# A fused attention, Fourier and feed-forward kernel: 13 plain attention tiles for 18, masking and weight conversion on VectorE, first Fourier rows placed by matrix products

## The chip, the cores and the metric

The kernel runs on one core of one Trainium2 chip. The metric is the device time of one execution in microseconds. The program has five engines that run beside one another, each with its own queue worked off in order: TensorE (PE; PEld is its weight load), VectorE (DVE), ScalarE (ACT), GpSimd (POOL) and the sync engine (SP), which here issues nearly all DMA transfers.

## The reference, cut to what matters

```python
# attention: 8 batches, 8 heads, 576 positions, head size 64, window of 64
scores = q @ k^T / 8, masked to 0 <= row - column < 64, else -1e9
attn = exp(scores - max) / (sum + 1e-9)
x = (attn @ v), heads put side by side          # (8, 576, 512)
# Fourier mixing and feed-forward
mixed = real(fft(fft(x, axis=1), axis=2))
u = x + mixed
un = (u - mean(u)) / sqrt(var(u) + 1e-6)
out = u + relu(un @ w_ch1) @ w_ch2              # w_ch1 512 x 2048, w_ch2 2048 x 512, float64
```

## The kernel before, in words

The 8 x 576 positions are 36 tiles of 128 rows (`NTT`); two batches make a pair of 9 tiles (`NT`). Each tile goes through `attn_tile`; when a batch is complete, `fft` transforms it, and `norm_tile` adds the Fourier rows to the attention rows and normalises them. Two tiles make a chunk, and `ffn` runs over 18 chunks.

**Plain and split tiles.** Tiles below `PRO` are plain (`whole`): scores and the product with v are float32 products, and k, q and the probabilities are transposed on PE against an identity (`flip`, L462; `flip_p`, L595). From `PRO` on, a tile is split into float16 high and low parts, multiplied in three passes or four partial products, and transposed by DMA (`k_turn`, `q_turn`, `p_turn`), with the splitting done on ACT, POOL or DVE. For a plain tile a product of an identity with the mask first puts the mask into the score bank (L542), four products add the scores (L545), DVE takes the row maximum (`top`, L573 and L574) and ACT the exponential from PSUM (L580). For a split tile DVE adds the mask and takes the minimum in one custom instruction a head pair (`masked`, L564).

**Order.** Every step is an `op` with an engine, a guessed duration and a priority. `Plan.order` simulates the engines with those guesses and writes out a fixed order for each queue: whatever can start first goes first, and priority settles ties. An attention tile has a base of 8.5 T plus an offset (`EARLY` for the first five); feed-forward products have 1e6 and more, so they fill PE where nothing else is ready. `slack` pretends that inputs of PE come later than planned. Where the plan sees PE idle before the first feed-forward product, `warm` products (L1265) fill the gap. A ring of ten `xu` tiles (`XR`) holds attention rows until their chunk is done, so tile T waits for chunk (T - 10) / 2.

**Weights.** The weights arrive as float64 words in 32 pieces of 512 KB (`weight_piece`, load L1069). A piece becomes float32 by integer steps: two on DVE (L1078, L1083), one on ACT (L1088), an addition on POOL (L1091); ACT then squares it for a scale (L1095). Chunk 0 is plain: it uses the float32 weights (`PLAIN = 1`). Later chunks use float16 high and low parts that `weight_split` makes once all pieces have been seen.

**Placing the first Fourier rows.** `fft` leaves its rows in three tiles `mp` by their index modulo 3, sends them to DRAM (`send`, L927), and later norm tiles gather them from there. For the first batch, tiles 0 and 1 don't go by way of DRAM:

```python
for T in range(2):
    ...
    for a0, a1 in ((j0, j0 + 32), (j0 + 32, j1)):
        r0 = cl + 3 * a0 - P * T
        nc.sync.dma_start(mts[T][r0 : r0 + 3 * (a1 - a0) - 2 : 3], t["mp", cl][a0:a1])
    op("DMA", 1.5, base + 5.25 + 0.01 * T, direct, [bmp], [Bmt[T]], lat=3.5)
```

Those are 12 transfers on SP (L944). `stats` of `norm_tile` (L992, L994) waits for them, then come `rstd`, `scale` (L1005), `flip` (L1017), and the first feed-forward products (L1186).

**Transposed Fourier input.** `radix4` (L680) folds a tile; for plain tiles and those with n in `Y_SOON` PE transposes it (`flip_y`, L739), for the others a DMA does (`y_turn`, L754).

Of the kernel before, what the change touches and what calls it, by code (L numbers as in the profile page):

```python
# [16 lines left out]
U32 = mybir.dt.uint32  # L17
AF = mybir.ActivationFunctionType
# [6 lines left out]
DM = H * D  # L25
# [270 lines left out]
def attn_fft_ffn_kernel(ctx: ExitStack, tc: tile.TileContext, q, k, v, w1, w2, gidx, dft_d, dft_s, mask, out):  # L296
# [27 lines left out]
    idb = cp.tile([P, P], BF16, name="idb")  # L324
# [30 lines left out]
    Bid, Bmh, Bmskb, Bgix, Bdd, Bds, Bones, Bidb = (Buf() for _ in range(8))  # L355
# [6 lines left out]
    op("POOL", 0.3, -499.5, lambda: nc.gpsimd.tensor_copy(idb, ident), [Bid], [Bidb])  # L362
# [15 lines left out]
    def to_parts():  # L378

        for i in range(2):  # L380
            fresh = i == PRO % 2
# [7 lines left out]
            op("POOL", 0.7, 100, ones, writes=[Bva[i], Bve[i]] if fresh else [Bva[i]])  # L389
# [21 lines left out]
    def attn_tile(T, base):  # L411
# [29 lines left out]
        kw = 512 if whole else 1024  # L441
        kst_ = (kst32 if whole else kst16)[:, T % 3 * kw : (T % 3 + 1) * kw].rearrange("p (h s) -> p h s", s=P)

        def keys(h, jj):
# [6 lines left out]
            own, old = T % 3 * w + 2 * h, (T - 1) % 3 * w + 2 * h + 1  # L451
# [21 lines left out]
        else:  # L473
# [57 lines left out]
        for jj in range(2):  # L531
# [5 lines left out]
            def score(jj=jj, m=m):  # L537
# [19 lines left out]
            rd = [Bq[i], bkT, *([] if jj or n == 0 else [BkT[(T - 1) % 3]])]  # L557
            op("PE", 1.15 if whole else 0.6, base + 2 + jj, score, [*rd, Bidb, Bmskb] if whole else rd, [bs, bp])
# [10 lines left out]
            def top(jj=jj):  # L569

                mx, nm = (sm.tile([P, 4], F32, tag=tag, name=f"{tag}{T}_{jj}") for tag in ("mx", "nm"))
                t["nm", jj] = nm
                nc.vector.tensor_reduce(out=mx, in_=t["ps", jj], axis=AX.X, op=ALU.max)  # L573
                nc.vector.tensor_scalar(out=nm, in0=mx, scalar1=-0.125, scalar2=None, op0=ALU.mult)  # L574
# [190 lines left out]

    def fft(b, base):
# [530 lines left out]
```

## Time and profile before

| what | value |
|---|---|
| device time, median of 3 runs | 1029.38 us (1027.97 to 1029.58) |
| the profiled execution's own time | 1027.26 us |
| its span, first to last instruction | 1025.4 us |
| mean granted TensorE clock | 0.994 |
| busy: PE, PEld | 989.6 us, 709.4 us |
| busy: DVE, ACT, POOL | 676.6, 416.9, 188.5 us |
| DMA moved | 115.83 MB, mean 113 GB/s |

The execution takes 1.86 us more than its span. A PE instruction's duration contains the way through the array, and neighbours overlap; what an operation costs a full PE is the time from its start to the start of what follows. Busy times of stretches count overlaps once; sums over groups of instructions count them twice. A float32 product has two records.

### The profile page before, as it was taken

The numbers are of one execution on the slowest core, as the hardware profiler recorded it, in microseconds if no ns is written. First come the engines' busy times: TensorE is split into PE (matmuls) and PEld (weight loads), VectorE is DVE, ScalarE is ACT, GpSimd is POOL, SyncE is SP. The second block draws the span as 40 slices with busy tenths as digits, with TensorE's granted clock in tenths as the row PEclk, the third lists the DMA queues.
The fourth block names the chain that finished last, engine by engine and source line by source line (L and its number), as shares of the span: only waits on it lengthen the run. The fifth ranks groups of instructions, "written<-read, shape, count | busy, mean of one in ns | idle before, by whom it ended". The sixth has DMA issues, their size and how long they took to land.

```text
span 1025.4 us, 22178 instructions
## 1 busy us (share of the span) xinstructions
PE 989.6 (97%) x8743; PEld 709.4 (69%) x8743; DVE 676.6 (66%) x1743; ACT 416.9 (41%) x1060; POOL 188.5 (18%) x200
## 2 busy tenths in 40 slices
PE   8788999999999999989999999999999999999998
PEld 7677767677776767666676676666676667666664
DVE  5799898798756495765775757778686754532121
ACT  5777766545424263233453225343453222211111
POOL 2124432121023020311123203032112100210000
PEclk9999999999999999999999999999999999999999
DMA  8979953337238156486798456686763511220000
GB/s 196 227 187 246 228 164 108 81 74 144 58 96 159 43 100 146 90 166 106 141 134 169 108 104 114 118 174 136 127 114 88 117 20 55 62 53 21 1 22 21
DMA packets 279032, 115.83 MB, mean 113 GB/s; under 512 B 260744, under 2 KB 260872, under 8 KB 278928
## 3 DMA queue, kind: packets, MB, share of 16 engines
q1 hardware_dynamic: 276208, 105.50, 49.9%
q0 software_dynamic: 2720, 8.92, 3.2%
q8 instruction: 69, 1.13, 0.5%
q14 instruction: 35, 0.29, 0.1%
HBM read 54.97 MB, written 14.17 MB: 67 GB/s over the span
## 4 chain that ended last, share of the span: by engine, by line
PE 71%; DVE 12%; DMA 10%; ACT 2%; SPq 2%; issue 2%; POOL 1%; DVEq 0%; ACTq 0%; POOLq 0%
PE ph L1186 31%; PE po L1167 28%; PE pa L646 2%; PE pz L899 2%; PE pg L867 2%; DMA uhl<-up 2%; DMA flex<-in_moe_w_ch 2%; DMA wd<-in_moe_w_ch 2%; PE psc L552 1%; DMA pt<-flex 1%; DVE y L680 1%; DMA va<-in_v 1%; DVE hh L1204 1%; DMA mt<-md,gix 1%; PE psc L545 1%
## 5 line engine op out<-in xcount | busy, mean ns | idle before, releaser
L1186 PE MATMUL ph<-uhl,w0s 128*128 128x256 f16 (+1 forms) x3384 | 426.6, 277 | 9.4 <-DVE hh L1204 9.2
L1167 PE MATMUL po<-w1s,hh 128*128 128x512 f16 (+1 forms) x1696 | 426.8, 389 | 0.0
L1186 PEld LDWEIGHTS <-w0s 128*128 128x128 f16 x3264 | 318.1, 98 | 94.9 <-issue 13.1
L1204 DVE SCALAR_TENSOR_TENSOR hh<-ph,hh 128x256 f16<-128x256 f32 x272 | 114.8, 423 | 235.3 <-ACT hh L1201 223.0
L1201 ACT ACTIVATE hh<-ph 128x256 f16<-128x256 f32 x272 | 104.0, 382 | 401.4 <-PE ph L1186 290.1
L1167 PEld LDWEIGHTS <-hh 128*128 128x128 f16 x1632 | 157.0, 98 | 138.3 <-issue 1.1
L977 POOL DMA_INDIRECT mt<-md,gix x34 | 34.3, 1008 | 111.3 <-DMA md<-mp 90.4
L1001 POOL TENSOR_TENSOR rs<-mv,mhalf 128x1 f32<-128x1 f32 x36 | 21.8, 606 | 178.2 <-DVE mv L997 161.5
L580 ACT ACTIVATE pr<-pr,nm 128x128 f32<-128x128 f32 x144 | 45.6, 390 | 5.7 <-DVE nm L564 5.7
L580 ACT ACTIVATE pr<-psc,nm 128x128 f32<-128x128 f32 x144 | 40.4, 380 | 16.6 <-DVE nm L574 12.5
L545 PEld LDWEIGHTS psc<-kst,qbd 128*128 128x128 f32 x288 | 37.5, 192 | 5.6 <-issue 1.7
L646 PE MATMUL pa<-ve,pt 128*64 128x65 f16 (+1 forms) x720 | 40.9, 209 | 0.1
L646 PE MATMUL pa<-va,pt 128*64 128x65 f16 (+1 forms) x720 | 40.5, 209 | 0.3 <-ACT pt L403 0.2
L545 PE MATMUL psc<-kst,qbd 128*128 128x128 f32 x288 | 38.4, 277 | 1.7 <-ACT qbd L403 1.2
L609 POOL TENSOR_TENSOR flex<-pr,flex 128x512 f16<-128x512 f32 x19 | 23.0, 1215 | 91.5 <-DVE flex L407 54.2
L482 POOL TENSOR_TENSOR flex<-kn,flex 128x512 f16<-128x512 f32 x15 | 17.6, 1176 | 117.8 <-ACT flex L403 92.3
L564 DVE CUSTOM_DVE_ANT_0 pr<-psc,mskb 128x128 f32<-128x128 f32 x144 | 32.8, 285 | 1.4 <-PE psc L552 1.4
L658 DVE TENSOR_TENSOR xu<-pa,rc 128x256 f32<-128x256 f32 x72 | 30.6, 425 | 2.5
L899 PE MATMUL pz<-g,ds__76 97*96 97x257 f16 (+3 forms) x240 | 29.1, 273 | 1.6 <-ACT pr L580 1.1
L680 DVE TENSOR_TENSOR y<-xu 128x256 f32<-128x256 f32 x66 | 29.7, 491 | 1.4 <-PE py L739 0.9
L899 PEld LDWEIGHTS <-ds__76 97*96 97x96 f16 (+1 forms) x240 | 26.8, 124 | 4.2 <-issue 2.6
L403 ACT CAST up<-un 128x512 f16<-128x512 f32 x28 | 17.2, 616 | 28.2 <-DMA uhl<-up 14.3
(155 smaller groups left out, 1214.9 us busy)
## 6 DMA issues: line engine op xcount, KB each, us to landing
wd<-in_moe_w_ch SPq DMA_DIRECT2D x20, 512.0 KB, 4.1
out<-xu SPq DMA_DIRECT2D x36, 256.0 KB, 2.4
ve<-va SPq DMA_DIRECT2D x68, 130.0 KB, 3.8
kn<-in_k SPq DMA_DIRECT2D x32, 256.0 KB, 4.1
qn<-in_q SPq DMA_DIRECT2D x32, 256.0 KB
flex<-in_moe_w_ch SPq DMA_DIRECT2D x12, 512.0 KB, 4.8
md<-mp SPq DMA_DIRECT2D x24, 192.0 KB, 2.7
va<-in_v SPq DMA_DIRECT2D x16, 256.0 KB, 5.4
```

The costliest lines, as they stand in the source:

```text
L545: nc.tensor.matmul(p_[:, hp], qw, keys(hp, jj), start=False, stop=(hp == 3))
L564: nc.vector.tensor_tensor_reduce(out=t["pr", jj][:, hp], in0=t["ps", jj][:, hp], in1=mskb[:, m : m + P], scale=-0.125, scalar=3.0e38, op0= ...
L580: nc.scalar.activation(pr, src, AF.Exp, bias=t["nm", jj][:, hp : hp + 1], scale=sc_)
L646: nc.tensor.matmul(pa[64 * jj : 64 * jj + 64, hh], pt[:, sl], v_, start=(x == 0), stop=(x == len(mm) - 1))
L658: nc.vector.tensor_tensor(out=xv[:, 4 * hf : 4 * hf + 4], in0=pa[:, :, 0:64], in1=rc.to_broadcast([P, 4, 64]), op=ALU.mult)
L680: eng.tensor_tensor(out=o, in0=p0, in1=p1, op=al)
L899: nc.tensor.matmul(pz[:M, c0:c1], ds_[:NJ, a, c[0] : c[0] + c[1]], t["g", gi][:, b_, c0:c1], start=(x == 0), stop=(x == len(mm) - 1),)
L977: nc.gpsimd.indirect_dma_start(out=mts[T], out_offset=None, in_=mds[pb][0 : HR if n < 4 else 2 * HR], in_offset=bass.IndirectOffsetOnAxis( ...
L1167: nc.tensor.matmul(t["po"][i], l_, r_, start=(f == 0 and x == 0), stop=(f == NKF - 1 and x == len(mm) - 1))
L1186: nc.tensor.matmul(ph, l_, r_, start=(x == 0), stop=(x == len(mm) - 1))
L1201: nc.scalar.activation(t["hh", f][:, 0], ph, AF.Relu)
L1204: nc.vector.scalar_tensor_tensor(out=hh[:, 1], in0=ph, scalar=0.0, in1=hh[:, 0], op0=ALU.max, op1=ALU.subtract)
```

## The change

- `PRO` 18 to 13: tiles 13 to 17 become split tiles. As 13 isn't the start of a pair, keys and values of tile 12 are converted once for tile 13 (`k_tail`, `v_next`, on DVE).
- Plain tiles lose the mask product; they use `masked` on DVE like the split ones, and ACT reads the probabilities from SBUF.
- The weights' ACT and POOL steps become one DVE instruction that adds into the low 16-bit half of each word.
- The 12 transfers become six float32 products with a matrix of ones and zeros (`place3`, made once on POOL), into two PSUM banks of the ring `f2`.
- `Y_SOON` loses n = 3; `LAZY` margins, priorities, pitch (8.5 to 10), `SLACK` (1.0 from tile 18 on, now 0.5 from tile 9 on) and the weights' priorities are other numbers.

```diff
-Y_SOON = (3,4,8,)
-LAZY, LAZY_FFT, LAZY_U = 0.2, 0.8, 0.2
-LAZY_E, LAZY_Y = 0.3, 0.4
+Y_SOON = (4, 8)
+LAZY, LAZY_FFT, LAZY_U = 0.2, 0.8, 0.5
+LAZY_E, LAZY_Y = 0.3, 0.8
-EARLY, LATER = 80, 0
-PRO = 18
-SLACK = 1.0
+EARLY, LATER = 60, -20
+PRO = 13
+PITCH, FFT_AT, NORM_AT, FFT1 = 10, 10, 9, 0
+SLACK = 0.5
-W_DMA, W_DMA_STEP, W_CONV, W_SQ, W_SPLIT, W_STEP = -40, 1.25, 40, 80, 60, 0.5
+W_DMA, W_DMA_STEP, W_CONV, W_SQ, W_SPLIT, W_STEP = -20, 1.6, 40, 60, 60, 0.5
...
+        if T == PRO and n > 0:
+            def k_tail():
+                ...
+            op("DVE", 1.6, base + 0.3, k_tail, [BkT[(T - 1) % 3]], [BkT[before], Buf("tail")])
...
-                if whole:
-                    nc.tensor.matmul(p_, idb, mskb[:, None, m : m + P].to_broadcast([P, 4, P]), start=True, stop=False)
-                    nc.tensor.matmul(p_[:, hp], qw, keys(hp, jj), start=False, stop=(hp == 3))
+                    nc.tensor.matmul(p_[:, hp], qw, keys(hp, jj), start=True, stop=True)
...
-            if whole:
-                op("DVE", 0.85, base + 2.1 + jj, top, [bs], [bnm], port=False)
-                op("ACT", 1.07, base + 2.5 + jj, expo, [bs, bnm], [bp])
-            else:
-                op("DVE", 0.86, base + 2.1 + jj, masked, [bs, Bmskb], [bp, bnm], port=False)
-                op("ACT", 1.2, base + 2.5 + jj, expo, [bnm], [bp])
+            op("DVE", 0.84, base + 2.1 + jj, masked, [bs, Bmskb], [bp, bnm], port=False)
+            op("ACT", 1.18, base + 2.5 + jj, expo, [bnm], [bp])
...
-                    op("DMA", 1.5, base + 5.25 + 0.01 * T, direct, [bmp], [Bmt[T]], lat=3.5)
+        for T in range(2 if b == 0 else 0):
+            def place(T=T):
+                mts[T] = bank("f2", f"mt{T}", (P, DM))
+                for cl, M in ((1, 96), (2, 96), (0, 97)):
+                    f0 = P * T + 2 - cl
+                    nc.tensor.matmul(mts[T], place3[0][:M, f0 : f0 + P], t["mp", cl][:M], start=(cl == 1), stop=(cl == 0))
+            op("PE", 2.6, base + 5.4 + 0.1 * T, place, [*bmps, Bplace], [Bmt[T]])
...
-                nc.scalar.mul(lo, lo.bitcast(U32), 2.0**-29)
-                nc.gpsimd.tensor_tensor(out=dst, in0=dst, in1=lo, op=ALU.add)
+                half_ = wf[x][g].bitcast(U16)[:, 0::2]
+                nc.vector.scalar_tensor_tensor(
+                    out=half_, in0=lo.bitcast(U32), scalar=2.0**-29, in1=half_, op0=ALU.mult, op1=ALU.add
+                )
...
-        base = 8.5 * T + (LATER if T > 4 else -EARLY)
-        plan.slack = SLACK if T >= PRO else 0.0
+        base = PITCH * T + (LATER if T > 4 else -EARLY)
+        plan.slack = SLACK if T >= NT else 0.0
```

## Rows read from the trace of the kernel before

**Rows 1.** The page: busy time and share of the span by engine
```profile
PE 989.6 (97%) x8743; PEld 709.4 (69%) x8743; DVE 676.6 (66%) x1743; ACT 416.9 (41%) x1060; POOL 188.5 (18%) x200
```
**Rows 2.** Stages: length, busy PE, PEld, DVE, ACT, POOL, clock, DMA share, GB/s
```profile
0.00:46.00 46.00, 37.62 (x350) 31.11 (x350) 30.70 (x77) 28.09 (x74) 8.74 (x18) 0.98 0.94 211
46.00:76.00 30.00, 24.90 (x287) 21.59 (x285) 26.95 (x63) 22.68 (x61) 7.37 (x7) 0.97 0.75 194
76.00:95.40 19.40, 15.75 (x160) 13.71 (x160) 18.14 (x44) 15.44 (x43) 8.21 (x7) 0.91 0.93 237
95.40:185.00 89.60, 86.33 (x560) 64.34 (x557) 77.47 (x154) 59.51 (x149) 32.07 (x25) 1.00 0.66 166
185.00:407.00 222.00, 219.02 (x1922) 159.80 (x1923) 157.45 (x398) 97.25 (x243) 35.90 (x41) 1.00 0.48 100
407.00:853.00 446.00, 437.64 (x4295) 304.48 (x4294) 313.79 (x892) 165.95 (x418) 87.27 (x91) 1.00 0.63 118
```
**Rows 3.** Groups of PE instructions, whole span: busy, mean ns, idle before
```profile
L1265 PE MATMUL warm<-ident 128*128 128x256 f16 x103 | 17.2, 314 | 1.3 <-POOL ident masks.py:199 1.3
```
**Rows 4.** The same, 76 to 95.4 us
```profile
L1265 PE MATMUL warm<-ident 128*128 128x256 f16 x24 | 4.3, 321 | 0.0
```
**Rows 5.** The same, 0 to 95.4 us
```profile
L542 PE MATMUL psc<-mskb,idb 128*128 128x512 bf16 x18 | 6.9, 381 | 0.1
```
**Rows 6.** PE in order of time, a plain tile: start, duration, what
```profile
259.86 0.39 PE L542 MATMUL psc<-mskb,idb 128*128 128x512 bf16 x1
260.09 1.05 PE L545 MATMUL psc<-kst,qbd 128*128 128x128 f32 x8
260.98 0.60 PE L462 MATMUL pk<-ident,kn 128*128 128x128 f32 x4
261.42 0.82 PE L1186 MATMUL ph<-uhl,w0s 128*128 128x256 f16 x6
```
**Rows 7.** Chain of waits, 0 to 110 us: start, duration, what
```profile
95.52 1.92 PE ph L1186 x8
...
100.48 1.08 PE pa L646 x32
```
**Rows 8.** PE in order of time, a split tile
```profile
502.19 0.22 PE L646 MATMUL pa<-ve,pt 128*64 128x65 f16 x1
...
502.60 0.62 PE L552 MATMUL psc<-kst,qbd 128*64 128x128 f16 x16
503.14 1.48 PE L1186 MATMUL ph<-uhl,w0s 128*128 128x256 f16 x12
```
**Rows 9.** PE in order of time, two float32 products of 512 columns
```profile
168.79 1.88 PE L1167 MATMUL po<-w1s,hh 128*128 128x512 f32 x4
170.51 0.70 PE L867 MATMUL pg<-dd,fs 128*128 128x65 f16 x12
```
**Rows 10.** Line 944, the placing transfers: ns min/median/max, first and last start
```profile
L944 SPq DMA_DIRECT2D mt<-mp x12: 530/678/922, 70.9 to 81.7; - x12
```
**Rows 11.** DVE in order of time: last mixing, first addition of Fourier rows
```profile
75.81 0.16 DVE L921 TENSOR_TENSOR mp<-pz,mp 97x3 f32<-97x3 f32 x1
...
86.92 0.69 DVE L992 TENSOR_TENSOR xu<-xu,mt 128x512 f32<-128x512 f32 x1
```
**Rows 12.** Groups of DVE instructions, 0 to 95.4 us: the plain tiles' maximum
```profile
L573 DVE TENSOR_REDUCE mx<-psc 128x4 f32<-128x512 f32 x18 | 12.3, 685 | 1.6 <-PE psc L545 1.6
L574 DVE TENSOR_SCALAR nm<-mx 128x4 f32<-128x4 f32 x18 | 6.6, 367 | 0.9
```
**Rows 13.** DVE in order of time: masking of a split tile, what follows
```profile
502.07 0.28 DVE L564 CUSTOM_DVE_ANT_0 pr<-psc,mskb 128x128 f32<-128x128 f32 x1
...
502.91 1.41 DVE L1224 SCALAR_TENSOR_TENSOR xu<-po,osc,xu 128x512 f32<-128x512 f32 x2
```
**Rows 14.** Line 1083, second DVE step of a weight piece
```profile
L1083 DVE SCALAR_TENSOR_TENSOR w1s<-wd,w1s x10: 682/693/1666, 68.6 to 178.5; 128x512 int32<-128x512 int32 x10
```
**Rows 15.** Line 1091, the addition on POOL
```profile
L1091 POOL TENSOR_TENSOR w1s<-w1s,wd x10: 1288/1356/1677, 69.5 to 179.3; 128x512 int32<-128x512 int32 x10
```

More of the change, by code (lines that the diff above doesn't have):

```diff
@@ L353, in attn_fft_ffn_kernel @@
     wp = [w_[:, 0:16].bitcast(F16).rearrange("p g (z c) -> p g z c", z=2) for w_ in ws]
-    Bid, Bmh, Bmskb, Bgix, Bdd, Bds, Bones, Bidb = (Buf() for _ in range(8))
+    Bid, Bmh, Bmskb, Bgix, Bdd, Bds, Bones = (Buf() for _ in range(7))
     Bq, Bva, Bve = ([Buf() for _ in range(2)] for _ in range(3))
@@ L380, in to_parts @@
         for i in range(2):
-            fresh = i == PRO % 2
+            fresh = PRO % NT == 0 and i == PRO % 2
             def ones(i=i, fresh=fresh):
@@ L387, in ones @@
                     nc.gpsimd.memset(ve[i][64:128], 0.0)
-            op("POOL", 0.7, 100, ones, writes=[Bva[i], Bve[i]] if fresh else [Bva[i]])
+            op("POOL", 0.7, PITCH * PRO - 25, ones, writes=[Bva[i], Bve[i]] if fresh else [Bva[i]])
     def pieces(src, b0, g0, n):
@@ L441, in attn_tile @@
         kw = 512 if whole else 1024
+        before = (T + 1 if T == PRO else T - 1) % 3
         kst_ = (kst32 if whole else kst16)[:, T % 3 * kw : (T % 3 + 1) * kw].rearrange("p (h s) -> p h s", s=P)
@@ L450, in keys @@
             w = kw // 64
-            own, old = T % 3 * w + 2 * h, (T - 1) % 3 * w + 2 * h + 1
+            own, old = T % 3 * w + 2 * h, before * w + 2 * h + 1
             step = old - own
@@ L505, in attn_tile @@
                 op("DMA", TURN, base + 0.7, lambda j=j: q_turn(j), Bfl[4:6], [Bq[i]], lat=2.8)
+        if T == PRO and n > 0:
+            def k_tail():
+                src = kst32[:, (T - 1) % 3 * 512 : (T - 1) % 3 * 512 + 512].rearrange("p (a s) -> p a s", a=4)
+                dst = kst16[:, before * 1024 : before * 1024 + 1024].rearrange("p (h s) -> p h s", h=H)
+                for h in range(2):
+                    old = src[64 * h : 64 * h + 64, :, 64:128]
+                    hi, lo = (dst[64 * z : 64 * z + 64, h::2, 64:128] for z in range(2))
+                    if h:
+                        odd = sb([P, 4, 64], F32, "tail", f"odd{T}")[0:64]
+                        nc.vector.tensor_copy(odd, old)
+                        old = odd
+                    nc.vector.tensor_copy(hi, old)
+                    nc.vector.tensor_tensor(out=lo, in0=old, in1=hi, op=ALU.subtract)
+            op("DVE", 1.6, base + 0.3, k_tail, [BkT[(T - 1) % 3]], [BkT[before], Buf("tail")])
         def v_part(z):
@@ L523, in v_next @@
         def v_next():
-            nc.sync.dma_start(vbuf[3 - i][64:128], vbuf[i][64:128])
+            if T + 1 == PRO:
+                (hi, lo), v_ = (ve[1 - i][64:128, z] for z in range(2)), va32[i][64:128]
+                nc.vector.tensor_scalar(out=hi, in0=v_, scalar1=VS, scalar2=None, op0=ALU.mult)
+                nc.vector.scalar_tensor_tensor(out=lo, in0=v_, scalar=VS, in1=hi, op0=ALU.mult, op1=ALU.subtract)
+            else:
+                nc.sync.dma_start(vbuf[3 - i][64:128], vbuf[i][64:128])
         op("DMA", 0.55, base - 4 if whole else base + 3.2, v_own, [Bva[i]], [Bve[i]], lat=2.8)
-        if n + 1 < NT:
+        if n + 1 < NT and T + 1 == PRO:
+            op("DVE", 1.1, base + 6, v_next, [Bva[i]], [Bve[1 - i]])
+        elif n + 1 < NT:
             op("DMA", 0.55, base - 3.9 if whole else base + 6, v_next, [Bva[i]], [Bve[1 - i]], lat=2.8)
@@ L555, in score @@
                             )
-            rd = [Bq[i], bkT, *([] if jj or n == 0 else [BkT[(T - 1) % 3]])]
-            op("PE", 1.15 if whole else 0.6, base + 2 + jj, score, [*rd, Bidb, Bmskb] if whole else rd, [bs, bp])
+            rd = [Bq[i], bkT, *([] if jj or n == 0 else [BkT[before]])]
+            op("PE", 0.95 if whole else 0.52, base + 2 + jj, score, rd, [bs, bp])
             def masked(jj=jj, m=m):
@@ L567, in masked @@
                     )
[L569 to L574, printed above, removed]
             def expo(jj=jj):
@@ L764, in attn_tile, with make_places @@
             op(*a, port=not soon)
+    Bplace, place3 = Buf("mt"), []
+    def make_places():
+        place3.append(sb([P, 258], F32, "mt", "place3"))
+        nc.gpsimd.memset(place3[0], 0.0)
+        nc.gpsimd.affine_select(
+            out=place3[0], in_=place3[0], compare_op=ALU.not_equal, fill=1.0, base=2, pattern=[[-1, 258]], channel_multiplier=3
+        )
+    op("POOL", 0.8, -60, make_places, writes=[Bplace])
     def fft(b, base):
@@ L1033, in norm_tile @@
             op("POOL", 1.0, base, gather, [*mdr, Bgix], [bmt], lat=2.6)
-        op("DVE", 1.13 + sum(0.75 if r else 0.6 for _, _, r in RANGES[n]), base + 0.5, stats, [bmt], [bx, bst])
+        op("DVE", 1.13 + sum(0.75 if r else 0.6 for _, _, r in RANGES[n]), base + 0.5, stats, [bmt], [bx, bst], port=T > 1)
         op("POOL", 0.54, base + 0.6, rstd, [bst, Bmh], [brs])
@@ L1102, in weight_piece @@
         op("DVE", 0.6, pr - 0.1, lambda: conv(1), bw, [bf])
-        op("ACT", 0.58, pr, lambda: conv(2), bw, [br])
-        op("POOL", 1.3, pr - 0.2, lambda: conv(3), [*bw, br], [bf])
+        op("DVE", 0.6, pr - 0.2, lambda: conv(2), bw, [bf])
         op("ACT", 0.72, W_SQ + W_STEP * order, square, [bf], [bj, Bssq[x]])
```

31 lines of the change are left out of this document (11 added, 20 removed).

## The prediction

> **What bounds the kernel now.** I read the page first: PE is busy 97% of the span, DVE 66% [rows 1]. A mean over stages hides limits, so the second view is the busy time by stage [rows 2]. The reader is to see two regimes. From 95.4 to 853 us PE is busy 742.99 of 757.6 us, 98%, at a granted clock of 1.00, and no other engine comes near: there a microsecond of PE work is a microsecond of time. Before 95.4 us PE is busy 78.27 us, but 17.2 us of that (an upper value, since neighbours overlap) are warm products that compute nothing [rows 3]. So up to 17.1 + 17.2 = 34.3 of 95.4 us are no work. DVE is the full engine there: 45.1 of 49.4 us from 46 to 95.4 [rows 2]. The third view, the chain of waits, gives the point where the regimes meet: the first feed-forward products start at 95.52 [rows 7]. PE's order in time then gives what each product costs a full PE, from its start to the start of the next.
>
> **The change part by part, against the profiled execution of 1027.26 us.**
>
> *Mask products.* One costs 260.09 - 259.86 = 0.23 us [rows 6]. Two for each of 18 plain tiles make 36; 18 of them run before 95.4 us [rows 5], where PE has spare time, and I count them as nothing (at best 4.1 us). The other 18 give -4.1 us. For them DVE masks: four instructions in 502.91 - 502.07 = 0.84 us [rows 13] where the maximum took 0.69 + 0.37 = 1.05 us [rows 12]. That is 0.21 us less a group, not more.
>
> *Tiles 13 to 17.* A plain tile without its masks costs PE two score steps of 260.98 - 260.09 = 0.89 us, four groups of transposes of 261.42 - 260.98 = 0.44 us [rows 6], and 1.08 us for the product with v [rows 7]: 1.78 + 1.76 + 1.08 = 4.62 us. A split tile costs two score steps of 503.14 - 502.60 = 0.54 us and two halves of 502.60 - 502.19 = 0.41 us [rows 8]: 1.90 us. Five tiles give 5 x 2.72 = -13.6 us. What it adds is for other engines: seven DMA transposes a tile (four for probabilities, two for q, one for k), splitting on ACT, DVE and POOL, and once `k_tail` and `v_next` on DVE, 2.7 us by the plan's own guess. All of it lies in 185 to 407 us, where DVE is 71% busy, ACT 44%, POOL 16% and the DMA share 0.48 [rows 2]; the feed-forward products hide it. Without that cover, PE would wait for a split tile's chain; the two ends are a loss of the whole 13.6 us and none. I take none, as the stage that already consists of split tiles (407 to 853 us) keeps PE busy 98% too.
>
> *Transposes of y.* Tiles 14, 15, 16, 21 and 30 leave PE: 5 x 0.44 = -2.2 us [rows 6]. The work of other engines is hidden as before.
>
> *Placing.* SP issues twelve transfers from 70.9 us on, 12 x 0.68 = 8.1 us of its queue, the last starting at 81.7 [rows 10]. The last of the rows that they move is written at 75.81 + 0.16 = 75.97 us [rows 11]; the first addition on DVE starts at 86.92 [rows 11], 10.95 us later. The change has six float32 products of 512 columns instead; two take 170.51 - 168.79 = 1.72 us [rows 9], so a tile's three take 2.6 us, and both tiles 5.2. The additions can start some 8 us earlier. The products run in a stretch where PE isn't full, so their 5.2 us cost nothing beyond their place in the chain (at worst all 5.2). What those 8 us are worth isn't 8: in 76 to 95.4 us PE was idle 3.65 us and warming 4.3 us [rows 2, 4], 41% of 19.4, and only that part is lost time; attention work that was done meanwhile is still to do. 8 x 0.41 = -3.3 us. SP's queue is also free of 8.1 us that weight and tile loads stood behind; I count nothing for it.
>
> *Weights.* The third step on DVE isn't in the trace. The nearest row is the second step, same kind and 512 columns: 0.69 us at the median, 1.67 us at most [rows 14]. I take 0.69 and keep both ends. The pieces come until 178.5 us [rows 14], so some 95.4 / 178.5 x 32 = 17 before chunk 0 starts: +11.7 us of DVE. Against it stand 18 x 0.21 = 3.8 us of masking saved and POOL additions of 1.36 us each [rows 15] that go. Net up to +7.9 us for a DVE that has 95.4 - 75.79 = 19.6 us idle there [rows 2]. I take nothing for it; at worst it pushes the start of chunk 0 back by 7.9 us and turns -3.3 into +4.6. The longest 1.67 us of a DVE step whose usual time is 0.69 fell in a stretch with such POOL additions, which is how a blocked instruction looks; how much comes back I leave out. The Trainium skill, "SBUF — State Buffer", section "Who interferes with whom", says that VectorE and GpSimd lock a shared port for whole instructions, and that a VectorE instruction with two SBUF inputs waits for a GpSimd one that reads SBUF. The 1.67 us agrees with it; by that rule up to an addition's time a piece, 1.36 us, would come back to DVE.
>
> A rule that speaks against this step: the Trainium skill, "Vector Engine (DVE) Microarchitecture Reference", section "Measured stream behaviour on trn2", has all three streams that leave their neighbours at every element at 1.98 ns a column, by which this step would take an estimated 1.09 us for 512 columns. The second step also reads every other word and takes 0.69 us, so the trace doesn't show the penalty on one stream; for three it is open.
>
> *Order.* Other priorities and slack rearrange the queues. Between 95.4 and 853 us PE idles 14.6 us; I take no change, with half of it, 7 us, either way.
>
> Sum: -4.1 - 13.6 - 2.2 - 3.3 = -23.2, so 1004.1 us for an execution like the profiled one. The median of the runs lies 2.1 us above that one; I add a part of it and predict 1005 us.
>
> **Rivals.**
>
> *A: the start gains more.* SP's free queue and DVE without POOL's additions let a third of the 34.3 lost us go: -11.4 in place of -3.3, so 1027.3 - 19.9 - 11.4 = 996 us. For it: DVE was the full engine and POOL ran 24.3 us beside it [rows 2]. Against it: DVE gets the third step.
>
> *B: the split tiles give back what PE saves.* If five more chains of transposes leave PE waiting for as much as it is spared, the 13.6 us go: 1027.3 - 4.1 - 2.2 - 3.3 = 1018 us. For it: a split tile passes through more engines. Against it: 98% in 407 to 853 us.
>
> *C, the other side: weights bound by DVE.* Chunk 0 needs all 32 pieces, and they last until 178.5 us. DVE is busy 153.3 of the first 185 us [rows 2]. If its 31.7 us of idle time are waits for loads that don't shrink, each third step moves the end of chunk 0 by its whole time. Then 32 x 0.69 = 22.1 us, less the 3.8 us of masking, is +18.3 against the 19.9 us spared later: 1026 us. It is slower than before from (19.9 + 3.8) / 32 = 0.74 us a step on; at 1.0 us, between the two ends of the row, +28.2 gives 1036 us. For it: DVE's share in the first stages. Against it: the POOL and ACT steps of a piece leave the same chain. By the rule on neighbouring elements, with its 1.09 us, C would give 1039 us.
>
> *D: the change does little.* If the masks were hidden too and B holds, only y and the placing stay, and with half of C's 18 us the time would lie at 1027 to 1031 us.
>
> **How the numbers follow.** Forecast 0.52, with a range of its own of 996 to 1014 (7 us of order and 2 of the run either way); A 0.17, B 0.17, D 0.05, C beyond its turning point 0.09. A difference of 0.2%, 2 us, is about what a measurement of this kernel can tell from none. Faster holds forecast, A and B: 0.86; same is D: 0.05; slower is C: 0.09. The range goes from A with order in its favour (996 - 7 = 989, less the 4.1 us of early masks counted at nothing, 985) to between B and C's lower price, 1021; it leaves out C, D and the edge of A.
>
> **What would show it.** The mask products are gone, and 26 plain groups of scores stand in place of 36. The addition of the first Fourier rows starts 3 us after their last mixing, in place of 11, and the first feed-forward product at about 87 us. The third weight step takes 0.69 us (C: 0.74 or more), and the last comes no later than 178 us; chunk 0's end tells C from the rest. From there to the end the time shrinks by some 20 us; if it shrinks by 6 only, with PE idle before scores or feed-forward products in 185 to 407 us, B is right. The forecast is wrong if chunk 0 starts after 95 us or if PE's busy share from then on falls below 97%.

## The result, and the profile after

The changed kernel takes 1017.76 us at the median (four runs, 1017.15 to 1019.02), the kernel before 1028.98 (1027.97 to 1029.58): a ratio of 0.9894, 95% interval 0.9876 to 0.9911, or 11.2 us less. The forecast was 1005 us, a gain of 24 us. The time lies inside the range of 985 to 1021, but at the price of rival B, 1018 us. The profiled execution took 1017.17 us with a span of 1015.3.

The page of the changed kernel, busy time by engine, answers to [rows 1]:

```profile
PE 972.7 (96%) x8756; PEld 687.3 (68%) x8756; DVE 679.6 (67%) x1979; ACT 417.9 (41%) x1047; POOL 197.4 (19%) x203
```

PE's share fell, from 97 to 96%, while the time fell too. So PE got less to do and waited for a larger share of its time. Its stages, with the columns of [rows 2]:

```profile
0.00:46.00 46.00, 38.23 (x378) 31.30 (x378) 32.54 (x148) 28.33 (x73) 3.98 (x15) 0.98 0.90 217
46.00:76.00 30.00, 26.99 (x258) 22.10 (x257) 26.24 (x87) 18.77 (x51) 1.39 (x3) 0.97 0.88 224
76.00:95.40 19.40, 17.45 (x127) 13.85 (x126) 18.35 (x45) 13.25 (x36) 1.76 (x2) 1.00 0.75 210
95.40:185.00 89.60, 84.75 (x586) 62.39 (x585) 79.97 (x225) 54.72 (x142) 6.20 (x7) 0.98 0.58 156
185.00:407.00 222.00, 213.92 (x2078) 150.43 (x2076) 172.82 (x499) 107.53 (x256) 69.82 (x63) 0.99 0.68 130
407.00:853.00 446.00, 432.87 (x4233) 300.01 (x4232) 303.94 (x869) 168.18 (x420) 100.70 (x98) 1.00 0.65 121
```

PE's idle time in 185 to 407 us is 222.00 - 213.92 = 8.1 us where it was 3.0, and in 407 to 853 us it is 13.1 where it was 8.4. In the first of these stages POOL went from 35.9 to 69.8 us, DVE from 157 to 173, the DMA share from 0.48 to 0.68. What PE waited for (us in total, times, the longest):

```profile
PE ph L1207 <- DVE hh L1225: 10.1, 10, 2.8
PE pa L657 <- DMA pt<-flex: 7.5, 4, 3.8
PE ph L1207 <- DVE wf L1111: 3.7, 1, 3.7
```

The first row has its like in the kernel before, 9.2 us in nine waits. The second is the changed kernel's own: the product with v waits for a DMA transpose of probabilities. In the kernel before, no product with v waited in its chunks 1 to 8.

**Work and lost time.** Busy time hides part of a loss, since records of neighbouring products overlap. So I count PE's work in a stretch: the number of products of each kind times their step at full clock, from start to start (a feed-forward product of 256 columns 0.109 us, of 512 columns 0.216 in 16-bit and 0.43 in float32, a plain score product 0.111, a split one 0.034, and so on). Warm products count as none. Lost time is the stretch's length less that, so it holds waits, warm products and what a lower clock costs; it is good to 1 or 2 us. A chunk ends where its second product's results begin to be added, and "start" ends with the first feed-forward product. "Changed again" is the same kernel in a second profile, the run after_again below.

```
lost us         work   lost | start  ch.0  ch.1-4  ch.5-8  ch.9-12
before         940.8   84.6 |  42.8   6.0    10.3     9.0     10.6
changed        922.5   92.8 |  35.5   9.6    14.5    17.8      9.7
changed again  922.7   93.3 |  33.6  11.0    15.3    20.9      6.7
```

The work fell by 18.3 us and the lost time grew by 8.2: together -10.1, the difference of the spans. Up to the end of chunk 4 the gain was 406.9 - 385.0 = 21.9 us; at the end of chunk 8 it was 604.4 - 593.7 = 10.7. Chunks 1 to 8 lost 32.3 us where they had lost 19.3. In the second profile of the changed kernel they lost 36.2, so a difference of some 4 us between two single profiles isn't one to build on.

### The profile page after: what moved, and what is told of

It reads as the page before. It is cut to its first block, busy times and chain, and to the rows that moved or that the text cites. A ratio compares the mean times of both kernels' runs of the same rounds, so it can differ in the third digit from the quotient of the medians.

```text
span 1015.3 us, 22449 instructions
## 1 busy us (share of the span) xinstructions
PE 972.7 (96%) x8756; PEld 687.3 (68%) x8756; DVE 679.6 (67%) x1979; ACT 417.9 (41%) x1047; POOL 197.4 (19%) x203
## 4 chain that ended last, share of the span: by engine, by line
PE 75%; DVE 8%; DMA 8%; SPq 5%; ACT 2%; issue 2%; POOL 0%; DVEq 0%; ACTq 0%; POOLq 0%
PE ph L1207 30%; PE po L1188 30%; PE pz L924 3%; PE pa L657 3%; DMA pt<-flex 2%; DMA kn<-in_k 2%; PE pg L890 2%; PE psc L568 2%; PE psc L575 2%; SPq L626 2%; SPq L499 1%; DVE y L691 1%; PE pp L606 1%; SPq L427 1%; DVE pr L587 1%
## 5 line engine op out<-in xcount | busy, mean ns | idle before, releaser
L1207 PE MATMUL ph<-uhl,w0s 128*128 128x256 f16 (+1 forms) x3384 | 427.1, 277 | 10.1 <-DVE hh L1225 10.1
L1207 PEld LDWEIGHTS <-w0s 128*128 128x128 f16 x3264 | 318.0, 98 | 97.6 <-issue 14.5
L595 ACT ACTIVATE pr<-pr,nm 128x128 f32<-128x128 f32 x288 | 90.9, 392 | 13.2 <-DVE nm L587 13.1
L587 DVE CUSTOM_DVE_ANT_0 pr<-psc,mskb 128x128 f32<-128x128 f32 x288 | 65.5, 285 | 15.3 <-PE psc L568 11.3
L1045 POOL TENSOR_TENSOR up<-un,up 128x512 f16<-128x512 f32 x33 | 39.7, 1204 | 75.8 <-ACT up L403 73.1
L620 POOL TENSOR_TENSOR flex<-pr,flex 128x512 f16<-128x512 f32 x23 | 27.4, 1190 | 133.8 <-ACT flex L403 93.5
L484 POOL TENSOR_TENSOR flex<-kn,flex 128x512 f16<-128x512 f32 x19 | 25.0, 1314 | 125.0 <-ACT flex L403 119.3
L403 ACT CAST flex<-pr 128x512 f16<-128x512 f32 x39 | 24.0, 615 | 23.5 <-DMA pt<-flex 21.1
L691 DVE TENSOR_TENSOR y<-xu 128x256 f32<-128x256 f32 x68 | 32.1, 512 | 0.6
L568 PE MATMUL psc<-kst,qbd 128*128 128x128 f32 x208 | 28.2, 282 | 3.1 <-ACT qbd L403 1.2
L657 PEld LDWEIGHTS <-pt 128*64 128x64 f16 x1104 | 20.7, 113 | 14.7 <-DMA pt<-flex 7.9
L495 POOL TENSOR_TENSOR flex<-qn,flex 128x1024 f16<-128x1024 f32 x12 | 26.2, 2187 | 16.3 <-ACT flex L403 14.1
```

The costliest lines, as they stand in the source:

```text
L568: nc.tensor.matmul(p_[:, hp], qw, keys(hp, jj), start=True, stop=True)
L587: nc.vector.tensor_tensor_reduce(out=t["pr", jj][:, hp], in0=t["ps", jj][:, hp], in1=mskb[:, m : m + P], scale=-0.125, scalar=3.0e38, op0= ...
L595: nc.scalar.activation(pr, pr, AF.Exp, bias=t["nm", jj][:, hp : hp + 1], scale=-1.0)
L657: nc.tensor.matmul(pa[64 * jj : 64 * jj + 64, hh], pt[:, sl], v_, start=(x == 0), stop=(x == len(mm) - 1))
L691: eng.tensor_tensor(out=o, in0=p0, in1=p1, op=al)
L1045: eng.tensor_tensor(out=t["up"][:, 1], in0=t["un"], in1=t["up"][:, 0], op=ALU.subtract)
```

## The experiments

Each run is compared with the kernel before, timed on the same chip. In the quoted texts, theory Q says that the split tiles' chains (16-bit parts made on POOL and DVE, DMA transposes issued by SP one after the other, products in PE's fixed order) return what PE saves; the rival S that the new slack and order numbers do.

**Thirteen plain tiles or eighteen** (pro18)

```diff
-PRO = 13
+PRO = 18
```

> The changed kernel with 18 plain tiles again; masking, weights, placing and order numbers as changed. Theory Q (five more split tiles crowd the queue of DMA transposes on SP, PE then waits for probabilities, and that eats what PE is spared): PE work grows by 13.6 us, lost time between 172 and 841 us falls by about as much, so 1014 to 1022 us, beside 1018 us of the changed kernel, and PE's wait for transposed probabilities before 440 us is gone. Rival S (the lost time comes from the lower slack and the other priorities, not from the split tiles): the work returns and the lost time stays, 1028 to 1034 us.

1019.35 us (1018.25 to 1021.65), 0.9929 [0.9903, 0.9954]. Its stage from 185 to 407 us, columns as above:

```profile
185.00:407.00 222.00, 222.00 (x1985) 162.72 (x1984) 155.35 (x484) 103.08 (x253) 41.26 (x46) 1.00 0.49 104
```

PE idles nowhere in it, where the changed kernel idles 8.1 us. In chunks 1 to 8 only one kind of wait is longer than 0.2 us:

```profile
PE ph L1207 <- DVE hh L1225: 5.5, 3, 3.3
```

The work is 15.2 us more (937.7), and chunks 1 to 8 lose 16.3 us in place of 32.3. So the five split tiles spare PE 15 us, and under the changed kernel's order some 16 are lost again in these chunks. By the whole time the two versions aren't told apart: the changed kernel's ratio was 0.9894, and 0.9928 when it was timed once more (after_again), beside 0.9929 here. The plain version loses 5 us more in chunks 9 to 12 (14.8). This is what Q says.

**Slack as before** (slack_one)

```diff
-SLACK = 0.5
+SLACK = 1.0
```

> The changed kernel with SLACK 1.0 in place of 0.5, still from tile 9 on. Rival S in its slack form: PE's waits for DVE and for DMA transposes after 172 us fall by 8 us or more, 1006 to 1011 us. Theory Q: SP's queue is as long as before, 1014 to 1021 us.

1015.5 us (1013.02 to 1019.68), 0.9908 [0.9876, 0.9940]; chunks 1 to 8 lose 30.7. Waits of PE:

```profile
PE ph L1207 <- DMA uhl<-up: 4.6, 1, 4.6
...
PE pa L657 <- DMA pt<-flex: 2.0, 1, 2.0
```

The wait for probabilities shrank from 7.5 to 2.0 us, and another took its place: the feed-forward product for its own transposed input. Slack moves the loss and doesn't remove it.

**All order numbers as before** (old_numbers)

```diff
-Y_SOON = (4, 8)
+Y_SOON = (3, 4, 8)
...
-EARLY, LATER = 60, -20
+EARLY, LATER = 80, 0
-PITCH, FFT_AT, NORM_AT, FFT1 = 10, 10, 9, 0
+PITCH, FFT_AT, NORM_AT, FFT1 = 8.5, 13, 6, 0
-SLACK = 0.5
+SLACK = 1.0
...
-        plan.slack = SLACK if T >= NT else 0.0
+        plan.slack = SLACK if T >= PRO else 0.0
```

The slack holds from the first split tile on, as before, which is tile 13 here.

> The changed kernel with all numbers of the order as they were (pitch, offsets, margins, slack, weights' priorities, n = 3 of y on PE); 13 plain tiles, masking, weights and placing as changed. Rival S: the numbers cost the gain, so 1003 to 1010 us. Theory Q: 1015 to 1024 us, with PE still waiting for transposed probabilities before 440 us.

1044.21 us (1041.06 to 1045.24), 1.0178 [1.0152, 1.0203]. The stage, and two of its waits on PE in order of time:

```profile
185.00:407.00 222.00, 201.39 (x1965) 142.25 (x1962) 168.87 (x479) 99.67 (x241) 47.43 (x44) 0.96 0.65 122
...
246.34 1.08 PE L750 MATMUL py<-ident,y 128*128 128x128 f32 x4 [5.49 <-DVE y L691]
...
255.36 0.26 PE L657 MATMUL pa<-va,pt 128*64 128x65 f16 x1 [6.89 <-DMA pt<-flex]
```

PE's work is the same but for two more transposes of y, 923.5 us, and 115.6 are lost. Neither theory expected that. S is reversed: the old numbers lose more, not less. The new numbers are worth some 26 us to this set of tiles by the times (1044.21 - 1017.76), 29 by the two ratios; the prediction had given the order 7 us either way.

That orders differ so much raises a rival: that the changed kernel's loss is chance of its order and not the five split tiles. PE's idle time from 185 to 407 us speaks against it. In seven planned orders with thirteen plain tiles (this run, the changed kernel, slack_one, and below transfers, weights_old, y_on_pe and late_lat) it is 7.3 to 20.6 us; in the three with eighteen (the kernel before, pro18, and below before_place) it is 0 to 6.1.

**The twelve transfers back** (transfers)

```diff
-            def place(T=T):
...
-                    nc.tensor.matmul(mts[T], place3[0][:M, f0 : f0 + P], t["mp", cl][:M], ...)
...
+                            nc.sync.dma_start(mts[T][r0 : r0 + 3 * (a1 - a0) - 2 : 3], t["mp", cl][a0:a1])
```

> The changed kernel with the first Fourier rows placed by 12 transfers on SP again, all else as changed. If the placing is worth what the start of chunk 0 shows (86.2 in place of 95.4 us, some 7 us less lost time before it): the first feed-forward product starts at 93 to 97 us and the time is 1021 to 1026 us. If the start moved for another reason (masks, weights off POOL): it starts before 90 us and the time stays within 1016 to 1020 us.

1028.96 us (1025.79 to 1035.1), 1.0020 [0.9998, 1.0043]. The stage ahead of chunk 0:

```profile
76.00:95.40 19.40, 14.04 (x99) 10.86 (x97) 18.49 (x52) 9.35 (x25) 2.30 (x3) 0.77 0.88 236
```

PE is busy 14.04 us of 19.40 where the changed kernel has 17.45, and its granted clock in this stretch is 0.77 in place of 1.00. PE stood 3.26 us up to 86.40 for a load of q; from 86.6 to 96.8 us the clock was at the lower of its two levels, 0.50 (1.2 GHz for 2.4), which cost some 5 of these 10.2 us (an estimate, from the two levels). The first feed-forward product starts at 91.6 us in place of 86.2, and 46.9 us are lost ahead of it in place of 35.5. But chunks 9 to 12 also lose 20.0 in place of 9.7, far from the edit: an undone part brings a newly planned order for everything behind it. The start and the time fit neither of the two cases expected, and the execution profiled was the longest of ten, 1035.1 us. What the placing is worth by itself isn't to be read from this run.

**Weights on three engines again** (weights_old)

```diff
-                nc.vector.scalar_tensor_tensor(
-                    out=half_, in0=lo.bitcast(U32), scalar=2.0**-29, in1=half_, op0=ALU.mult, op1=ALU.add
-                )
+                nc.scalar.mul(lo, lo.bitcast(U32), 2.0**-29)
+                nc.gpsimd.tensor_tensor(out=dst, in0=dst, in1=lo, op=ALU.add)
```

> The changed kernel with the third weight step on ACT and POOL again. If the DVE step is about neutral, as forecast (chunk 0 ends 3 us late for it, and DVE gets its time back from POOL): lost time up to the end of chunk 0 within 4 us of the changed kernel's 45 us, 1014 to 1022 us. If POOL's additions held DVE back for a good part of their 44 us: chunk 0 ends 8 us or more later, 1025 to 1035 us.

1026.3 us (1022.41 to 1030.69), 0.9993 [0.9973, 1.0013]. Waits of PE:

```profile
PE ph L1207 <- DMA uhl<-up: 7.0, 1, 7.0
PE ph L1207 <- POOL w0s L1112: 3.7, 2, 2.7
```

Chunk 0 ends at 179.9 us in place of 176.7, and chunks 0 to 4 lose 15.4 + 22.4 us in place of 9.6 + 14.5. With its order planned anew, going back costs 7 to 10 us by the ratios (0.9993 beside 0.9928 and 0.9894); about 3 of these are at the end of chunk 0, where the addition on POOL is waited for. The time is the one expected for the second case, the end of chunk 0 is nearer to the first.

**All transposes of y on PE** (y_on_pe)

```diff
-Y_SOON = (4, 8)
+Y_SOON = tuple(range(9))
```

> The changed kernel with every tile's y transposed on PE: 17 DMA transposes, some 21 us, leave SP's queue, and 17 x 0.44 = 7.5 us come to PE. Queue theory (SP's time to issue transposes is what PE waits for): lost time in chunks 1 to 8 falls from 32 us by 10 or more, 1008 to 1017 us. Rival (the way of a split tile through ACT, POOL and DVE is what PE waits for, whatever SP does): lost time stays, 1022 to 1027 us.

1020.77 us (1017.53 to 1025.55), 0.9927 [0.9902, 0.9952]: 17 x 0.44 = 7.5 us more work, lost time in chunks 1 to 8 29.2 in place of 32.3. The time lies between the two theories; taking these transposes from SP gives little back.

**Loads and stores from ACT's queue** (loads_act)

```diff
-                nc.sync.dma_start(t[nm][o : o + m], ap)
+                (nc.sync if whole else nc.scalar).dma_start(t[nm][o : o + m], ap)
...
-            op("DMA", 0.75, -11, lambda g=g: nc.sync.dma_start(of[P * g : P * g + P], xts[g]), ...)
+            op("DMA", 0.75, -11, lambda g=g: nc.scalar.dma_start(of[P * g : P * g + P], xts[g]), ...)
```

> The changed kernel with the loads of q, k and v of split tiles and all output stores issued from ACT's queue, so that SP holds transposes and copies of v only; the planned order is the same. Queue theory: SP's issue time from 240 to 600 us falls by 30 us or more, PE's wait for transposed probabilities goes, 1005 to 1013 us. Rival (the way through the engines): 1015 to 1021 us, or slower where ACT waits in front of a transfer.

1014.01 us (1011.96 to 1017.69), 0.9868 [0.9827, 0.9910]. Counted transfer by transfer, SP issues for 401 us in all in place of 471, and from 240 to 600 us for 208 in place of 245: the cut that was wanted. But chunks 1 to 8 still lose 27.2 us, and PE's wait is hardly shorter:

```profile
PE pa L657 <- DMA pt<-flex: 6.4, 5, 2.9
```

The time lies between the two theories. It is the lowest so far of a kernel that leaves nothing out, but its interval overlaps that of the changed kernel; the two aren't told apart.

**Placing alone, in the kernel before** (before_place)

```diff
+                for cl, M in ((1, 96), (2, 96), (0, 97)):
+                    nc.tensor.matmul(mts[T], place3[0][:M, f0 : f0 + P], t["mp", cl][:M], ...)
...
-                            nc.sync.dma_start(mts[T][r0 : r0 + 3 * (a1 - a0) - 2 : 3], t["mp", cl][a0:a1])
```

> The kernel before with the placing by products alone; 18 plain tiles, mask products, weights and numbers as before. If the placing by itself takes some 7 us of lost time away before chunk 0: first feed-forward product at 86 to 90 us, 1018 to 1024 us. If it needs the other parts (DVE is full without them): first product after 92 us, 1026 to 1031 us.

1037.41 us (1036.67 to 1039.79), 1.0094 [1.0057, 1.0130]. The feed-forward products (count; ns at least, median, most; first and last start):

```profile
L1196 PE MATMUL ph<-uhl,w0s x3384: 269/273/483, 89.0 to 1023.8; 128*128 128x256 f16 x192, 128*128 128x256 f32 x8
```

The start does come earlier, 89.0 in place of 95.4 us, and 7.8 us less are lost ahead of it. But the work grows by the 5.2 us of the six products, chunks 0 to 4 lose 8.8 more, and the kernel is slower, outside both ranges. Alone, with the old numbers and the order that they give here, the placing isn't a gain.

**The changed kernel once more** (after_again): an edit of nothing, for the runs below.

> The changed kernel again, beside the three others of this set: ratio to the kernel before 0.987 to 0.992.

1018.51 us (1015.36 to 1026.53), 0.9928 [0.9897, 0.9959], just above what was expected; its account is in the table above.

**ACT's queue and slack together** (loads_act_slack)

```diff
-SLACK = 0.5
+SLACK = 1.0
...
+                (nc.sync if whole else nc.scalar).dma_start(t[nm][o : o + m], ap)
```

> The changed kernel with split tiles' loads and the stores on ACT's queue, and slack 1.0. If both small gains (lost time 89.1 and 88.1 us beside 92.8) stand beside each other: 1004 to 1011 us, ratio 0.978 to 0.984. If they are one and the same wait, or chance of the order: 1010 to 1018 us.

1013.85 us (five of six 1010.53 to 1014.42, one 1026.42), 0.9869 [0.9818, 0.9920]; chunks 1 to 8 lose 31.0. The two gains don't add. It is faster than the kernel before, but by no more than with ACT's queue alone.

The next three keep the planned order of every engine as in the changed kernel and only take real work out of it, so that what they return isn't a new order's. They act on all split tiles from 14 or 15 on, not only on the five that the change adds.

**No transposes of q from tile 15 on** (no_q_turn): the scores of these tiles use an older q.

```diff
-                op("DMA", TURN, base + 0.7, lambda j=j: q_turn(j), ...)
+                op("DMA", TURN, base + 0.7, lambda j=j: q_turn(j) if T < PRO + 2 else None, ...)
```

> The changed kernel in the same order, from tile 15 on without the two DMA transposes of q; the scores of those tiles use an older q. Queue theory: 42 transposes, some 55 us of SP's queue, are gone, so lost time in chunks 1 to 8 falls from 32 us to 22 or less, 1003 to 1010 us. Rival (the subtractions on POOL and DVE, which PE's inputs stand behind): 1013 to 1018 us.

1001.23 us (1000.72 to 1002.59), 0.9753 [0.9694, 0.9811]. Stages:

```profile
185.00:407.00 222.00, 217.48 (x2127) 153.21 (x2126) 174.42 (x509) 108.45 (x260) 71.72 (x64) 1.00 0.62 118
407.00:853.00 446.00, 440.92 (x4303) 306.93 (x4301) 309.22 (x875) 169.95 (x430) 101.15 (x98) 1.00 0.51 104
```

Chunks 1 to 8 lose 17.3 us in place of 32.3, though POOL and DVE do all that they did. It isn't SP's issuing time alone that came back: from 185 to 407 us SP issues for 112 us here, 110 in loads_act and 131 in the changed kernel, and loads_act got back 5 us, not 15 (there ACT issued the loads, which may have cost it part). What else went with the transposes of q is the time until they land and the buffers that they hold until then: from 185 to 600 us ACT's conversions to high parts waited 9.3 us for transposes of q and 14.1 us for those of probabilities in the changed kernel, 1.1 and 5.8 us here.

**Low parts for one head only, from tile 14 on** (lo_small): the subtractions for the low parts of k, q and the probabilities are left out for the other heads; every transpose stays.

```diff
-                    eng.tensor_tensor(out=lo, in0=src, in1=hi, op=ALU.subtract)
+                    few = slice(0, H if T == PRO else 1)
+                    eng.tensor_tensor(out=lo[:, few], in0=src[:, few], in1=hi[:, few], op=ALU.subtract)
...
```

> The changed kernel in the same order, with the subtractions for the low parts of k, q and the probabilities done for one head or head pair only from tile 14 on; the rest of the low parts stays as it was. SP's transposes are all there. Queue theory: time within 4 us of the changed kernel, 1012 to 1018 us. Rival (POOL's and DVE's subtractions): POOL loses some 70 of 197 us, lost time in chunks 1 to 8 falls to 22 us or less, 1002 to 1009 us.

1005.44 us (1003.95 to 1006.05), 0.9797 [0.9739, 0.9856]. Stages:

```profile
185.00:407.00 222.00, 218.65 (x2134) 154.02 (x2131) 163.12 (x510) 109.75 (x263) 42.98 (x64) 1.00 0.71 134
407.00:853.00 446.00, 437.91 (x4292) 305.50 (x4290) 282.35 (x874) 169.02 (x428) 73.68 (x97) 1.00 0.65 120
```

Chunks 1 to 8 lose 19.1 us, with SP's transposes all there. Either cut alone returns 13 to 15 us: neither the transposes nor the subtractions on POOL and DVE alone are the bound.

**Both cuts** (both_small): the two edits above together.

> The changed kernel in the same order with both cuts: no DMA transposes of q from tile 15 on, low parts of k, q and probabilities for one head or head pair only from tile 14 on. If either cut frees an engine that PE waited for by itself, the two add up: lost time in chunks 1 to 8 from 32 to 36 us down to 5 us or less, 988 to 995 us. If both shorten one and the same chain, which the order has room for once it is short enough: lost time stays at 14 to 18 us, 997 to 1002 us.

995.64 us (994.61 to 998.4), 0.9680 [0.9654, 0.9705]. Stages:

```profile
185.00:407.00 222.00, 220.91 (x2159) 156.20 (x2157) 164.67 (x512) 110.31 (x265) 43.84 (x64) 1.00 0.59 120
407.00:853.00 446.00, 443.05 (x4323) 308.88 (x4321) 284.81 (x880) 169.41 (x428) 76.01 (x98) 1.00 0.51 103
```

Chunks 1 to 8 lose 10.8 us, 21.5 less than the changed kernel; the single cuts give 15.0 + 13.2 = 28.2. So they are, it seems, links of one chain in part, and in part separate delays; by the ratios, beside 0.9928, the cuts return 18, 13.5 and together 25.5 us, less than their sum too. The loss is now below the 19.3 us of the kernel before, which also has split tiles in its later chunks: the chains cost something there too.

**Truer landing times in the plan** (late_lat)

```diff
-            op("DMA", TURN, base + 0.2, k_turn, [bkp], [bkT], lat=2.0)
+            op("DMA", TURN, base + 0.2, k_turn, [bkp], [bkT], lat=3.2)
...
-            op("DMA", HTURN, base + 4.2 + jj, lambda g=p_turn: g(0), [bpp], [bt, bt2], lat=1.8)
+            op("DMA", HTURN, base + 4.2 + jj, lambda g=p_turn: g(0), [bpp], [bt, bt2], lat=3.0)
...
```

> The changed kernel with the plan's landing times of DMA transposes raised by 1.0 to 1.4 us (k 2.0 to 3.2, q 2.8 to 4.2, probabilities 1.8 to 3.0, y and u 2.2 to 3.2); nothing else. If PE waits since the chain of a split tile takes longer than the plan has it: lost time in chunks 1 to 8 falls by 8 us or more, 1004 to 1011 us. If the order is as good as it gets and the chain itself is too long: 1013 to 1021 us.

1044.93 us (1041.82 to 1047.25), 1.0170 [1.0140, 1.0200]. Waits of PE:

```profile
PE ph L1207 <- DMA uhl<-up: 23.9, 3, 13.6
PE py L750 <- DVE y L691: 10.0, 5, 6.9
```

A miss for both theories. Chunks 1 to 8 lose some 2 us less than in the changed kernel, and what is behind them some 27 us more: there the feed-forward products now wait up to 13.6 us for their inputs. Why the longer landing times made that order wasn't followed up.

**The same, with ACT's queue** (late_lat_act): the edits of late_lat and loads_act together.

> The same landing times, with split tiles' loads and the stores on ACT's queue: 3 to 5 us below the run with the landing times alone if the shorter SP queue counts, equal to it otherwise.

1051.73 us (1051.01 to 1052.23), 1.0229 [1.0203, 1.0255]. A miss as well.

## Why the prediction was right or wrong

**The failed step** is the one for tiles 13 to 17: "What it adds is for other engines ... the feed-forward products hide it ... the two ends are a loss of the whole 13.6 us and none. I take none". The loss is about the whole. Chunks 1 to 8 lose 13.0 us more than before; with eighteen plain tiles they lose 16 less. PE's busy share from 95.4 to 853 us fell from 98.1 to 96.6% (84.75 + 213.92 + 432.87 of 757.6 us), below the 97% that was to show the forecast wrong. And from the end of chunk 0 to the last instruction the time shrank by 840.7 - 838.6 = 2.1 us, where some 20 were forecast and 6 go with B; part of what the start gained is attention work that now comes later. Rival B named the mechanism and its price; it had a chance of 0.17. That its 1018 us are met so closely is partly luck: the start gained 2.9 us more than B's sum has, and chunk 0 lost 3.6.

How the chain works can be followed at one of its waits. SP in order of time in the changed kernel (start, duration, what):

```profile
349.75 1.25 SPq L765 DMA_TRANSPOSE py<-yp  x1
351.43 1.21 SPq L626 DMA_TRANSPOSE pt<-flex  x1
352.69 1.31 SPq L499 DMA_TRANSPOSE qbd<-flex  x1
354.06 1.95 SPq L487 DMA_TRANSPOSE kst<-flex  x1
356.05 2.60 SPq L626 DMA_TRANSPOSE pt<-flex  x2
358.70 1.32 SPq L499 DMA_TRANSPOSE qbd<-flex  x1
360.06 1.14 SPq L427 DMA_DIRECT2D kn<-in_k  x1
361.25 1.32 SPq L626 DMA_TRANSPOSE pt<-flex  x1
```

From 351.43 to 362.57 us SP issues without a gap longer than 0.12 us: transposes of probabilities, q and k, and a load between them. DVE and POOL make the last parts of probabilities meanwhile (conversion to high parts, subtraction for the low ones):

```profile
358.79 0.43 DVE L407 CAST flex<-pr 128x512 f16<-128x512 f32 x1 [2.95 <-DMA pt<-flex]
359.35 1.15 POOL L620 TENSOR_TENSOR flex<-pr,flex 128x512 f16<-128x512 f32 x1 [10.18 <-DVE flex L407]
```

PE in order of time, over the end of that:

```profile
361.33 0.64 PE L575 MATMUL psc<-kst,qbd 128*64 128x128 f16 x16
361.90 0.20 PE L657 MATMUL pa<-ve,pt 128*64 128x65 f16 x1
365.85 0.26 PE L657 MATMUL pa<-va,pt 128*64 128x65 f16 x1 [3.76 <-DMA pt<-flex]
```

The wait is made of several links. DVE's conversion stands until 358.79 us for a buffer that an earlier transpose of probabilities still holds; that one had its turn on SP at 356.05, behind transposes of q and k. The subtraction ends at 360.50. SP is then at a load of k, and the last transpose has its turn at 361.25. PE comes to the product that needs it at 362 and stands until 365.85, with feed-forward products behind it in its fixed order: 4.6 us after the turn, where a transpose of probabilities took 2.8 us at the median from issue to landing in the kernel before.

SP's queue has more in it throughout. From 240 to 360 us, counted transfer by transfer in stretches of 40 us, it issued for 28.8 + 29.0 + 30.2 = 88.0 us with 46 transposes in the changed kernel, for 10.4 + 15.3 + 12.3 = 38.0 us with 14 before, and for 41.6 us with 18 in the version with eighteen plain tiles. Nothing there is full: SP issues for 73% of these 120 us, and POOL is busy 31% of 185 to 407 us. That is why a look at busy shares found cover. What counts is the chain's length, in which every link can stand behind others' work, against PE's place for the product. The no_q_turn and lo_small runs show it: with the same order, shortening either link in all split tiles from 14 or 15 on returned 13 to 15 us.

The argument for no loss was that 407 to 853 us, where all tiles are split, keeps PE busy 98%. Idle time of 8.4 us is small in 446, but both cuts together bring the lost time of chunks 1 to 8 below that of before: that stage wasn't free of the cost either. And the loss doesn't stay where the five tiles are: 8.8 of the 13.0 us that chunks 1 to 8 lose more, by a count good to 1 or 2 us, fall into chunks 5 to 8, from 385 to 594 us, where both kernels have split tiles. What part of that comes from the five tiles' chains and what from the new order there, the runs don't tell; pro18, with an order of its own, loses some 6 us less in chunks 5 to 8.

**Right: PE's work.** Forecast -4.1 - 13.6 - 2.2 = -19.9 us later, -4.1 of early masks, +5.2 for placing: -18.8. Counted: -18.3. The changed kernel has 208 / 8 = 26 plain groups of scores; in the kernel before it was 288 / 8 = 36, with 36 mask products.

**Right in direction, larger: placing and the start.** The changed kernel, last mixing, placing products, first addition, first feed-forward product:

```profile
69.56 5.32 PE L967 MATMUL mt<-mp,place 96*128 96x512 f32 x12
69.66 0.16 DVE L946 TENSOR_TENSOR mp<-pz,mp 97x3 f32<-97x3 f32 x1
72.42 0.67 DVE L1013 TENSOR_TENSOR xu<-xu,mt 128x512 f32<-128x512 f32 x1
...
86.25 2.11 PE L1207 MATMUL ph<-uhl,w0s 128*128 128x256 f32 x9
```

The addition starts 72.42 - 69.82 = 2.6 us after the last mixing (forecast 3; before, 10.95 [rows 11]), and chunk 0 starts at 86.2 us (forecast about 87). Twelve records in 5.32 us are the six products, at the 5.2 worked out from [rows 9]. What that was worth ahead of chunk 0: 7.3 us less lost, 5.2 of placing, -4.1 of masks: -6.2, where -3.3 was forecast. Chunk 0 gave 3.6 of it back.

That chunk 0 starts where it was forecast is partly luck, and its gain isn't the placing's alone. The last mixing itself ends 75.97 - 69.82 = 6.15 us earlier, which the prediction didn't have; from the first addition to the first product it takes 86.25 - 72.42 = 13.8 us, where it took 8.5, since attention work stands between. And the granted clock from 76 to 95.4 us is 1.00, where it was 0.91 before [rows 2]: there PE had idled 2.28 us up to 85.22, and the clock was at the lower of its two levels, 0.50, from 85.07 to 88.48 us, worth some 1.7 us (an estimate, from the 0.91). No run parts these three.

**Weights: C's price at its turning point, and no more.** The third step (ns at least, median, most; first and last start):

```profile
L1111 DVE SCALAR_TENSOR_TENSOR w1s<-wd,w1s x10: 733/742/756, 81.7 to 170.6; 128x512 uint16<-128x512 uint32 x10
```

0.74 us, not the 0.69 taken. The Trainium skill, "Vector Engine (DVE) Microarchitecture Reference", section "Measured stream behaviour on trn2", would have it at an estimated 1.09 us, if the row for streams that hop 4 KiB at every 32-bit element held for this step, whose streams go on by one or two words: this run doesn't show that penalty. 0.74 is where C breaks even, but its condition failed: the last step starts at 170.6 us (178 was the bound) and chunk 0 ends at 176.7 in place of 184.7. PE waits for a piece once, 3.7 us on L1111, as much as chunk 0's added loss. Without POOL's additions the second step never takes over 0.693 us, where it had taken up to 1.67 beside one [rows 14]. That agrees with the Trainium skill, "SBUF — State Buffer", section "Who interferes with whom", by which the two engines lock a shared port. Going back to three engines cost 7 to 10 us (weights_old): this part seems worth more than the nothing that I took, but that figure holds another planned order too.

**Order: its range was too small.** 7 us either way were given. With the same PE work to 1 us, old_numbers and late_lat lose some 23 to 24 us more than the changed kernel. That is what an order can cost this set of tiles; what the new numbers did within the change itself no run parts from the rest.

**What stays open.** How the 16 us divide between SP's queue, the landing of transposes, the buffers that they hold and the subtractions: cut singly, the transposes of q and the subtractions return 15 and 13, together 21.5, in all split tiles and not in the five alone. Also whether before's order numbers, chosen anew, would make eighteen plain tiles better, and whether ACT's queue is a gain on top.

The sum, by the account: later work -19.4, start -6.2, chunk 0 +3.6, chunks 1 to 8 +13.0, the rest -1.1: -10.1 us.

## What to carry to other kernels

Count the bound engine's work and its lost time apart, stage by stage: the first could be forecast here to a microsecond from counts and steps, while the second was put at nothing and came out at 13 us; work moved to other engines is hidden only if its whole chain (each link with what stands ahead of it in its queue) ends before the bound engine's fixed order needs it. Busy shares of 30 to 75% didn't show that here. Where a planner orders everything, undoing a part tests that part and a new order together; to test a cause, keep the order and take the real work away, and compare two cuts that take the same time from one queue (loads_act and no_q_turn) before calling that queue the cause.

## What the runs showed of the hardware

A DMA transpose of probabilities or of q holds SP's queue for 1.3 us at the median, and up to 2.6. The two kinds in the changed kernel, 185 to 407 us (ns at least, median, most):

```profile
L626 SPq DMA_TRANSPOSE pt<-flex x26: 1193/1276/2272, 254.4 to 405.6; - x26
...
L499 SPq DMA_TRANSPOSE qbd<-flex x18: 1241/1312/2587, 228.9 to 396.0; - x18
```

Seven a tile at some 1.3 us are 9 us of SP for each split tile. And the third weight step, whose three streams all take every second element (32-bit words in, 16-bit halves in and out), costs DVE 0.05 us more for 512 columns than the second step, 0.74 beside 0.69.
